# Attention with memory slots, a two-layer net and four experts: another layout for a softmax, and a new issue order

## The chip, the cores and the metric

The kernel runs on one core of a Trainium2 chip, as one launch. The metric is the device time of that launch in microseconds (us). The kernel before took 1147.62 us (median of 3 runs, 1147.52 to 1148.19). Five engines work side by side, each through its own queue strictly in order: TensorE (PE, with PEld for its weight loads), VectorE (DVE), ScalarE (ACT), GpSimd (POOL), and SyncE (SP), which here only issues DMAs. Results of PE land in PSUM; everything else lives in SBUF.

## The reference, cut to what matters

```python
# 4 batches x 8 heads, 576 tokens, head size 64, 32 memory slots
a = exp(phi - max over tokens); a /= sum over tokens + 1e-9      # first softmax, per head and slot
k_m, v_m = a^T k, a^T v                                          # 32 x 64 per head
scores = q k_m^T / 8;  attn = softmax over the 32 slots          # second softmax, per token
x = attn v_m                                                     # (2304 tokens, 512)
h = x @ w_in;  x = (max(h,0) + alpha*min(h,0)) @ w_out           # 512 -> 2048 -> 512 ("first layers")
p = domain_probs / sum
out = sum over 4 experts e of p[:, e] * (max(x @ w1[e], 0) @ w2[e])   # 512 -> 1024 -> 512
```

## The kernel before, in words

Precision first, since it sets how much PE has to do: most products are made of three passes in a fast fp32 type, with each operand split into a high part (a cast, on ACT) and a low part (the rest, `sub_to`, L140, on DVE or POOL). A product of two 128-wide blocks with 288 token columns is therefore three matmuls, and every operand has a "hi" and a "lo" that must exist before it.

The work falls into four stages.

- **Attention** (L160 to L321), per batch b and half g of the heads (4 heads x 32 slots = 128 partitions). `att_max`, `att_exp`, `att_sum` are the first softmax over the tokens, with phi laid out slots by tokens. `att_nat` turns the exponentials into the tokens' layout (four PE transposes a half and two more for the last 64 tokens), `att_natc` copies them out of PSUM on ACT, `att_mem` makes k_m and v_m from them, `att_memc` scales them by 1/sum, `att_memt` and `att_memtc` transpose those, `att_score` gives the scores of 288 tokens, `att_evac` takes them into the tokens' layout. Class `Soft` (L267) is the second softmax: max, sub, exp, sum, mul, back, and a split.
- **First layers** (class `First`, L446): 128 steps (c, b, k, f): `up` (L463 or L466) makes 128 hidden units of 288 tokens, `relu` and `act` apply the slope, `fin` and `fin2` split, `down` (L497 or L500) adds them to four PSUM banks, `evac` adds the banks to y. w_in and w_out arrive as integers' halves and are put together by class `Decode`; v_m is folded into w_in (`fold`), so that attention's last product and w_in are one.
- **Experts, batches 0 and 1**, then **batches 2 and 3**: 8 groups g of 512 hidden units. `Up` makes the hidden block of a unit by seven block products in place of eight (p1 to p7, L700), with sums v1, v16, v167 and blocks c11 to c22 between; `gate` applies max and p; `hi` and `lo` split; `Down` or `Seven` (L791, L831) makes the output. Weight splits made in the first half (`w1_hi`, `w1_lo`, `w2_split`, `s_sum`, `s_part`) are stored to HBM and loaded in the second.

What sets the order: everything is issued by hand. `ORDER` (L29) is a list of task names; each is one function call, and an instruction stands on its engine's queue where its task stands in the list. After the list, `run_experts` (L898) issues the experts by a fixed rule: around each product of a unit it calls `extra(place)` for the weight work of that place. `ON_VECTOR` (L95) names the low parts, subtractions and decode steps that go to DVE; the others go to POOL. `warm` (L148) issues matmuls on the identity whose result nobody reads; there are 42 of them, in tasks w0 to w3, all before the first transposes. Buffers come from pools with fixed counts: six PSUM banks for attention, sums and y (`ps_a`), two for hidden blocks and outputs (`ps_h`), three for raw weights (`rawp`), so a load or a product also waits until its buffer's last reader is done.

Of the kernel before, what the change touches and what calls it, by code (L numbers as in the profile page):

```python
# [8 lines left out]
F32 = mybir.dt.float32  # L9
# [15 lines left out]
NG = E * F // 512  # L25
UNIT = 4 * S
# [3 lines left out]
ppr w3 w1 w2 p0 a00_max rin0 rin1 w0 a00_exp a00_sum a01_max pal kv0 in0_1 in0_0 in1_1 pgates a01_exp a01_sum in1_0  # L30
in1_2 in1_3 in1_4 a00_nat a00_natc in0_2 a01_nat a01_natc a01_nath a01_nathc a00_mem p1 a00_memc a10_max a01_mem
a00_memt a01_memc a01_memt a01_memtc q0 a01_sc0 a11_max a00_memtc a00_sc0 a11_exp a01_ev0 s010_max in0_3 in0_4 f000
s010_sub s010_exp q01 a00_sc1 a01_sc1 a00_ev0 s000_max s000_sub a11_sum rin2 in2_1 in2_0 in2_2 in2_3 a10_exp a11_nat
# [71 lines left out]
def memory_attention_experts(ctx: ExitStack, tc: tile.TileContext, phi, q, kv, w_in, w_out, w1, w2, alpha, dp, out):  # L105
# [63 lines left out]
    def load_q(b, hf=None):  # L169
        if not hf:  # L170
            q_t[b] = unit(f"q{b}")
# [1089 lines left out]
```

## Time and profile before

| | |
|---|---|
| median of 3 runs | 1147.62 us |
| the profiled execution: its own time | 1150.11 us |
| its span, first to last instruction | 1148.3 us |
| PE busy | 1128.2 us, 98% |
| DVE, POOL, ACT busy | 72%, 42%, 38% |
| mean granted TensorE clock | 0.991 of full |
| attention and first layers | to about 388 us |
| experts, batches 0 and 1; 2 and 3 | to about 797 us; to the end |

"Busy" for PE is a share of time in which some matmul was under way, not the share of its peak. Matmuls are pipelined, so 12 of them show 1.6 us while one alone shows 0.3. A better measure of lost time in a stretch is how many matmuls of the same shape it held.

### The profile page before, as it was taken

The page shows a single profiled execution, that of the slowest core. Times are in us where ns is not written, and L with a number is a line of the kernel's source. Part 1 is how long each engine was busy: PE and PEld are TensorE (multiplying, and loading weights), DVE is VectorE, ACT ScalarE, POOL GpSimd, SP SyncE. Part 2 cuts the span into 40 slices and gives each one's busy share as a digit, 9 for nine tenths or more (in the row PEclk, how much of TensorE's full clock was granted, in tenths as well). Part 3 has the DMA queues.
Part 4 walks back from the last instruction along what each step waited for, and adds up shares of the span by engine and source line. Part 5 has one row for each costly group of instructions (what it writes and reads, how often), then busy time and mean ns, then how long its engine had stood idle before and what let it go on. Part 6 is the DMA issues. An engine that isn't in the chain of part 4 may idle for free.

```text
span 1148.3 us, 21977 instructions
## 1 busy us (share of the span) xinstructions
PE 1128.2 (98%) x8708; PEld 1086.3 (95%) x8708; DVE 822.8 (72%) x1498; ACT 441.0 (38%) x914; POOL 485.7 (42%) x395
## 2 busy tenths in 40 slices
PE   8999999999999989999999999999999999999998
PEld 7578999999999889999999999999999999999998
DVE  5998878675676565775766757687577777777794
ACT  4667644443444344333333333333532222222220
POOL 3345444342244574564745547333323333333320
PEclk9999999999999989999999999999999999999999
DMA  9552222111021273663745637585464555556522
GB/s 379 196 239 61 68 80 75 38 38 37 2 85 54 76 268 149 240 236 112 285 154 224 231 140 271 204 292 190 155 184 151 182 173 178 166 167 185 166 66 73
DMA packets 64214, 180.02 MB, mean 157 GB/s; under 512 B 6640, under 2 KB 23024, under 8 KB 60400
## 3 DMA queue, kind: packets, MB, share of 16 engines
q1 hardware_dynamic: 64112, 178.63, 45.0%
q8 instruction: 68, 1.11, 0.4%
q14 instruction: 34, 0.28, 0.1%
HBM read 114.34 MB, written 64.26 MB: 156 GB/s over the span
## 4 chain that ended last, share of the span: by engine, by line
PE 86%; DVE 5%; issue 1%; POOL 1%; DMA 1%; ACT 1%; DVEq 0%; ACTq 0%; POOLq 0%
PE o L808 18%; PE y L500 16%; PE c L872 13%; PE uy L700 12%; PE h L466 8%; PE ux L700 8%; PE uw L700 8%; PE pw L425 1%; PE y L497 1%; DVE g L140 1%; DMA kv<-in_kv 1%; POOL w L140 0%; POOL g L140 0%; DVE h L778 0%; PE pm L228 0%
## 5 line engine op out<-in xcount | busy, mean ns | idle before, releaser
L808 PE MATMUL o<-g,w 128*128 128x288 f32 x1536 | 225.8, 296 | 0.6 <-DVE g L140 0.3
L808 PEld LDWEIGHTS o<-g,w 128*128 128x128 f32 x1536 | 211.7, 189 | 1.1 <-DVE g L140 0.6
L500 PE MATMUL y<-g,wout 128*128 128x288 f32 x1440 | 207.3, 297 | 2.2 <-DVE g L140 1.9
L500 PEld LDWEIGHTS y<-g,wout 128*128 128x128 f32 x1440 | 196.5, 189 | 9.4 <-DVE g L140 2.4
L700 PE MATMUL uy<-x,w 128*128 128x288 f32 x1152 | 186.4, 297 | 2.9 <-DVE v L734 2.9
L700 PEld LDWEIGHTS uy<-x,w 128*128 128x128 f32 x1152 | 164.1, 189 | 5.3 <-DVE v L734 5.3
L872 PE MATMUL c<-gc,w2c 128*128 128x288 f32 x1008 | 156.5, 295 | 0.5 <-ACT acc L885 0.5
L140 POOL TENSOR_TENSOR gc<-h,gc 128x576 fp32r<-128x576 f32 x56 | 82.9, 1488 | 143.6 <-ACT gc L859 98.6
L872 PEld LDWEIGHTS c<-gc,w2c 128*128 128x128 f32 x1008 | 141.2, 188 | 1.0 <-ACT acc L885 1.0
L700 PE MATMUL ux<-x,w 128*128 128x288 f32 x768 | 124.2, 298 | 2.8 <-ACT v L738 2.8
L700 PE MATMUL uw<-x,w 128*128 128x288 f32 x768 | 122.7, 295 | 0.0
L140 POOL TENSOR_TENSOR g<-act,g 128x288 fp32r<-128x288 f32 x67 | 57.6, 863 | 140.8 <-ACT g L485 117.4
L700 PEld LDWEIGHTS ux<-x,w 128*128 128x128 f32 x768 | 110.2, 190 | 3.3 <-ACT v L738 3.3
L466 PE MATMUL h<-a,wp 128*128 128x288 f32 x720 | 111.2, 297 | 0.0
L140 POOL TENSOR_TENSOR w<-raww,w 128x512 fp32r<-128x512 f32 (+1 forms) x48 | 76.7, 1613 | 76.8 <-ACT w L602 49.8
L700 PEld LDWEIGHTS uw<-x,w 128*128 128x128 f32 x768 | 109.0, 188 | 0.0
L466 PEld LDWEIGHTS h<-a,wp 128*128 128x128 f32 x720 | 99.9, 188 | 7.5 <-DVE act L481 2.8
L859 ACT CAST gc<-h 128x576 fp32r<-128x576 f32 x70 | 47.3, 676 | 151.8 <-DVE h L851 138.4
L825 DVE TENSOR_TENSOR acc<-o,acc 128x288 f32<-128x288 f32 x112 | 50.8, 454 | 69.1 <-PE o L808 69.1
L481 DVE SCALAR_TENSOR_TENSOR act<-neg,bet,h 128x288 f32<-128x288 f32 x120 | 59.9, 510 | 52.3 <-ACT neg L472 45.3
L734 DVE TENSOR_TENSOR v<-uy,v 128x288 f32<-128x288 f32 x128 | 58.2, 454 | 53.2 <-PE uy L700 53.1
L472 ACT ACTIVATE neg<-h 128x288 f32<-128x288 f32 x128 | 52.1, 412 | 94.0 <-PE h L466 90.1
(164 smaller groups left out, 1611.4 us busy)
## 6 DMA issues: line engine op xcount, KB each, us to landing
kw<-w SPq DMA_DIRECT2D x16, 1792.0 KB, 6.7
raww<-in_w SPq DMA_DIRECT2D x32, 512.0 KB, 4.2
w<-kw SPq DMA_DIRECT2D x32, 512.0 KB, 4.8
kS<-S SPq DMA_DIRECT2D x56, 256.0 KB, 4.4
w2c<-kS SPq DMA_DIRECT2D x28, 512.0 KB, 3.6
kw<-w SPq DMA_DIRECT2D x25, 512.0 KB, 2.6
w<-kw SPq DMA_DIRECT2D x48, 256.0 KB, 4.0
kv<-in_kv SPq DMA_DIRECT2D x8, 1152.0 KB, 8.2
```

The source lines that it names most:

```text
L140: eng.tensor_tensor(out=out, in0=in0, in1=in1.bitcast(F32), op=ALU.subtract)
L425: mm(pw_t[b, c, u, n0][32 * t:32 * t + 32, 0:n1 - n0], vt_t[b, u][r, 32 * t:32 * t + 32], win_t[c][r, t, n0:n1], start=True, stop=True,)
L466: mm(p, wp_t[b, c, g][:, x, fs], a_t[b][:, y, g, o:o + HB], start=(n == 0), stop=(n == 5))
L472: nc.scalar.activation(out=self.neg, in_=self.p, func=AF.Relu, scale=-1.0)
L481: nc.vector.scalar_tensor_tensor(out=self.g, in0=self.neg, scalar=bet[:, ft:ft + 1], in1=self.p, op0=ALU.mult, op1=ALU.add)
L500: mm(First.acc[d], w[:, x, d * 128:(d + 1) * 128], self.gt[:, y, 0:HB], start=(self.start and n == 0), stop=(self.stop and n == 2))
L700: mm(p, w[:, x, a, k], operand(self.b, i)[:, y, k], start=(start and n == 0), stop=(n == 5), skip_group_check=not start)
L734: nc.vector.tensor_tensor(out=out, in0=x, in1=y, op=ALU.add)
L808: mm(self.p, w[:, x, i, d % 2 * 128:(d % 2 + 1) * 128], g, start=(m == 0), stop=(m == 11), skip_group_check=len(hps) == 1)
L825: nc.vector.tensor_tensor(out=a, in0=self.p, in1=a, op=ALU.add)
L859: nc.scalar.copy(out=t[:, 0], in_=self.raw[q])
L872: mm(self.p, w[:, x, i, m * 128:(m + 1) * 128], self.g_t[q][:, y, i], start=(k == 0), stop=(k == 5))
```

## The change

Three things, and an order that is new almost everywhere before the experts' second group and near the end.

1. For batches 2 and 3 (`b >= TURNED`), phi is loaded twice: in the slots' layout as before (into the other half of the buffer) and in the tokens' layout (`load_nat`, a host-side rearrangement of the same numbers). The column of negated maxima is turned into a row by one PE transpose a half (`att_row`), DVE adds it to the tokens' layout (`att_less`, one operand in PSUM), and ACT takes the exponential there (`att_nat`). The ten transposes a batch and their copies go. `att_exp` stays, for the sum.
2. For batches 1 to 3 the scores of both halves g are one task (`att_scores`); instructions are the same.
3. `run_experts` becomes `plan_experts`, which lists the same calls as named tasks, cut finer (`w1_lo` in two, a store apart from its split). `ORDER` now reaches into that list: the first expert units of groups 0 and 1 and the last ones of groups 5 to 7 are written out in `ORDER`; what stands between them keeps the old rule's order. `ON_VECTOR` is drawn anew. `bet`'s slope correction is a task of its own (`slopes`), and the combination of the seven products may run on POOL.

Warm-up matmuls are 72 in place of 42, in 24 tasks of three. By kind, the built program has on PE 20 transposes of exponentials fewer (40 to 20), 4 of maxima more, and 30 warm-ups more. DVE loses 29 instructions (1500 to 1471), POOL gains 37 (400 to 437), ACT 2, SP two DMAs (phi's second layout, 576 KB each). Of what goes from DVE to POOL, most is four `sub` and four `mul` of 128 x 576 and one of each of 128 x 288 in the second softmax, and five w_in products (with five more ACT conversions).

The diff, cut to its core (the two tables are shown by two lines each):

```diff
@@ ORDER, ON_VECTOR
-ppr w3 w1 w2 p0 a00_max rin0 rin1 w0 a00_exp a00_sum a01_max pal kv0 in0_1 in0_0 in1_1 pgates a01_exp a01_sum in1_0
+w1 w3 w0 w5 w18 p0 a01_max a00_max w8 w20 a01_exp a01_sum w17 a00_exp rin2 w14 w12 ppr in2_0 in2_1 w11 a00_sum rin0
...
+x1h5 e123 sp2 h126 h127 to x1l5 x1l6 p1_000 v1_000 wh01 l127 wl010 d124 d125 vh011 v16_000 x1h2 x1h4 l126 wl011 x1l2
@@ loads
     def load_phi(b):
-        pe_t[b] = unit(f"pe{b}")
-        nc.sync.dma_start(out=pe_t[b][:, 0:S2], in_=phi[b])
+        if b not in pe_t:
+            pe_t[b] = unit(f"pe{b}")
+        o = 0 if b < TURNED else S2
+        nc.sync.dma_start(out=pe_t[b][:, o:o + S2], in_=phi[b][:, S2:])
+
+    def load_nat(b):
+        if b not in pe_t:
+            pe_t[b] = unit(f"pe{b}")
+        nc.sync.dma_start(out=pe_t[b][:, 0:S2], in_=phi[b][:, 0:S2])
@@ first softmax (att_nat, att_natc of before are now att_turn, att_turnc, for b < 2)
+    def att_row(b, g):
+        p = pn_t[b, g] = bank(f"pn{b}{g}")
+        nc.tensor.transpose(p[:, 0:128], stats[b, g][1].to_broadcast([128, 128]), ident)
+
+    def att_less(b, g):
+        pe, p = pe_t[b], pn_t[b, g]
+        x = pe[:, g * 512:(g + 1) * 512].rearrange("p (c m) -> p c m", c=4)
+        nc.vector.tensor_tensor(out=x, in0=x, in1=p[:, 0:128].rearrange("p (c m) -> p c m", c=1).to_broadcast([128, 4, 128]), op=ALU.add)
+        r = slice(64 * g, 64 * g + 64)
+        nc.vector.tensor_tensor(out=pe[r, 1024:1152], in0=pe[r, 1024:1152], in1=p[r, 0:128], op=ALU.add)
+
+    def att_nat(b, g):
+        x = pe_t[b][:, g * 512:(g + 1) * 512]
+        nc.scalar.activation(out=x, in_=x, func=AF.Exp, scale=1.0)
...
+    def att_scores(b, hf):
+        for g in range(2):
+            att_score(b, g, hf)
@@ experts
-    def w1_lo(g, hp):
-        for (w, src), eng in zip(w1_parts(g, hp), (nc.gpsimd, nc.vector)):
-            sub_to(eng, w[:, 1], src, w[:, 0])
-        raw_t.pop(("w1", 2 * g + hp))
...
+    def w1_lo(g, hp, i):
+        w, src = w1_parts(g, hp)[i]
+        sub_to(engine(f"wl{g}{hp}{i}"), w[:, 1], src, w[:, 0])
...
-    def run_experts():
+    def plan_experts():
+
+        plan = []
+
+        def do(name, fn, *args):
+            plan.append((name, fn, args))
...
-    for i, n in enumerate((11, 12, 6, 13)):
-        task(f"w{i}", warm, n)
+    for i in range(24):
+        task(f"w{i}", warm, 3)
...
+    plan = plan_experts()
+    for name, fn, args in plan:
+        task(name, fn, *args)
...
         for name in ORDER.split():
             run(name)
-        run_experts()
+        for name, fn, args in plan:
+            if name in tasks:
+                run(name)
```

Three places of the new order, since the tables tell a reader little. **SP at the very start** (pe0 is phi of batch 0, rawin and rawout are chunks of w_in and w_out, kv00 and kv01 keys and values of batch 0). Before:

```order
L1123 DMA pr_104<-in_dp 128x72
L162 DMA pe0_150<-in_phi 128x1152
L335 DMA rawin0_155<-in_w_in 128x1024
L335 DMA rawin1_157<-in_w_in 128x1024
L1123 DMA bet_103<-in_alpha 128x16
L167 DMA kv00_178<-in_kv 128x2304
L167 DMA kv01_179<-in_kv 128x2304
L162 DMA pe1_246<-in_phi 128x1152
L173 DMA q0_286<-in_q 128x1152 x2
L335 DMA rawin2_340<-in_w_in 128x1024
L167 DMA kv10_380<-in_kv 128x2304
L167 DMA kv11_381<-in_kv 128x2304
```
Now:

```order
L331 DMA pe0_135<-in_phi 128x1152
L532 DMA rawin2_159<-in_w_in 128x1024
L1410 DMA pr_104<-in_dp 128x72
L532 DMA rawin0_180<-in_w_in 128x1024
L532 DMA rawin1_199<-in_w_in 128x1024
L1410 DMA bet_103<-in_alpha 128x16
L341 DMA kv00_253<-in_kv 128x2304
L341 DMA kv01_254<-in_kv 128x2304
L331 DMA pe1_280<-in_phi 128x1152
L347 DMA q0_322<-in_q 128x1152
L532 DMA rawin3_348<-in_w_in 128x1024
L347 DMA q0_322<-in_q 128x1152
```
A third w_in chunk stands ahead of the keys and values, and further on batch 1's keys and values now follow five loads that came after them before (a fourth w_in chunk, two of w_out's and both layouts of batch 2's phi: three of 512 KB and two of 576 KB).

**DVE where the first layers end** (act3313, g3313 are the last step's hidden block and its low part, y33100 to y33103 its sums; w101 is the second half of the first w1 block; v16000 and v167000 sums of the first expert unit). Before:

```order
L481 SCALAR_TENSOR_TENSOR act3313_4928<-neg3313_4894,bet_103,h3313_4880 128x288
L140 TENSOR_TENSOR w101_4986<-s01_4318,w101_4986 128x1024
L140 TENSOR_TENSOR g3313_4954<-act3313_4928,g3313_4954 128x288
L511 TENSOR_TENSOR y3_1782<-y33100_4912,y3_1782 128x288
L511 TENSOR_TENSOR y3_1782<-y33101_4913,y3_1782 128x288
L511 TENSOR_TENSOR y3_1782<-y33102_4914,y3_1782 128x288
L511 TENSOR_TENSOR y3_1782<-y33103_4915,y3_1782 128x288
L734 TENSOR_TENSOR v16000_5036<-uy000_5027,v1000_5034 128x288
L734 TENSOR_TENSOR v167000_5059<-uy000_5027,v1000_5034 128x288
L734 TENSOR_TENSOR h000_5051<-uw000_5038,v167000_5059 128x288
```
Now:

```order
L669 SCALAR_TENSOR_TENSOR act3313_4926<-neg3313_4923,bet_103,h3313_4909 128x288
L699 TENSOR_TENSOR y3_1815<-y33000_4847,y3_1815 128x288
L699 TENSOR_TENSOR y3_1815<-y33001_4848,y3_1815 128x288
L699 TENSOR_TENSOR y3_1815<-y33002_4849,y3_1815 128x288
L699 TENSOR_TENSOR y3_1815<-y33003_4850,y3_1815 128x288
L307 TENSOR_TENSOR x16_4900<-y1_1227,x16_4900 128x576
L307 TENSOR_TENSOR g3313_4960<-act3313_4926,g3313_4960 128x288
L307 TENSOR_TENSOR w101_5003<-raww11_3950,w101_5003 128x768
L921 TENSOR_TENSOR v16000_5038<-uy000_4828,v1000_5001 128x288
L307 TENSOR_TENSOR w101_5003<-s01_4368,w101_5003 128x1024
L699 TENSOR_TENSOR y3_1815<-y33100_5008,y3_1815 128x288
L699 TENSOR_TENSOR y3_1815<-y33101_5009,y3_1815 128x288
```
The low part of w101 stood ahead of the low part g3313 that the last `down` needs; now it stands behind it, cut in two, with the first expert sum between.

**ACT in the first expert units** (v1000, v1001, v1010 copy a first product out of PSUM, h000, h001 a block, g000, g001 are the high parts, w2000 to w2011 high parts of w2, S100 and S200 high parts of w2's sums). Before:

```order
L738 COPY v1000_5034<-ux000_5020 128x288
L753 COPY h000_5051<-ux000_5020 128x288
L784 CAST g000_5077<-h000_5051 128x576
L738 COPY v1001_5094<-ux001_5062 128x288
L784 CAST g000_5077<-h000_5051 128x576
L753 COPY h001_5114<-ux001_5062 128x288
L406 CAST w2000_5116<-raww20_4526 128x512
L406 CAST w2010_5121<-raww21_5017 128x512
L653 CAST S100_5137<-S10_5126 128x512
L653 CAST S200_5154<-S20_5141 128x512
L738 COPY v1010_5186<-ux010_5172 128x288
L784 CAST g001_5188<-h001_5114 128x576 x2
```
Now:

```order
L758 CAST x14_5041<-xt1_4710 128x576
L861 CAST w2000_5074<-raww20_5070 128x512
L861 CAST w2001_5076<-raww20_5070 128x512
L861 CAST w2010_5078<-raww21_4772 128x512
L758 CAST x14_5041<-y1_1227 128x576
L944 COPY h000_5101<-ux000_4994 128x288
L925 COPY v1001_5153<-ux001_5124 128x288
L834 CAST S100_5169<-S10_5072 128x512
L944 COPY h001_5199<-ux001_5124 128x288
L925 COPY v1010_5221<-ux010_5138 128x288
L976 CAST g000_5234<-h000_5101 128x576
L976 CAST g001_5236<-h001_5199 128x576
```
The copy v1010 stood behind two parts of w2's sums; now one part stands ahead of it, and the high parts of w2 stand ahead of h000 and v1001.

## Rows read from the trace of the kernel before

**Rows 1.** The page, part 1: busy time, share, instructions.

```profile
PE 1128.2 (98%) x8708; PEld 1086.3 (95%) x8708; DVE 822.8 (72%) x1498; ACT 441.0 (38%) x914; POOL 485.7 (42%) x395
```

**Rows 2.** Stretches: length; PE, PEld, DVE, ACT, POOL busy; clock, DMA share, GB/s.

```profile
20.00:30.00 10.00, 7.68 (x118) 4.48 (x105) 9.36 (x27) 5.89 (x17) 3.83 (x5) 0.69 1.00 418
30.00:40.00 10.00, 8.66 (x73) 5.29 (x73) 8.34 (x20) 5.02 (x15) 2.86 (x4) 0.80 0.33 120
40.00:100.00 60.00, 58.23 (x506) 43.65 (x507) 56.63 (x107) 40.22 (x97) 26.00 (x23) 1.00 0.54 199
...
380.00:420.00 40.00, 33.76 (x216) 32.52 (x215) 25.08 (x34) 14.62 (x29) 24.58 (x17) 0.87 0.54 200
450.00:470.00 20.00, 19.37 (x143) 18.83 (x142) 17.26 (x21) 8.52 (x17) 15.40 (x12) 1.00 0.86 322
510.00:740.00 230.00, 230.00 (x1730) 229.30 (x1729) 155.61 (x257) 76.27 (x133) 130.62 (x106) 1.00 0.54 203
1100.00:1120.00 20.00, 18.86 (x139) 18.18 (x138) 19.15 (x35) 4.43 (x9) 2.86 (x2) 1.00 0.06 20
```

**Rows 3.** Waits of PE, 376 to 412 us: waiter, releaser, total, times, longest.

```profile
PE ux L700 <- ACT v L738: 2.8, 1, 2.8
PE y L500 <- DVE g L140: 1.9, 1, 1.9
PE uy L700 <- DVE v L734: 1.5, 2, 0.9
```

**Rows 4.** Timeline of DVE, 364 to 386 us: start, us, line, operation, count, idle.

```profile
369.67 0.46 DVE L140 TENSOR_TENSOR g<-act,g 128x288 fp32r<-128x288 f32 x1 [0.50 <-ACT g L485]
...
381.60 2.05 DVE L140 TENSOR_TENSOR w<-s,w 128x1024 fp32r<-128x1024 f32 x1 [2.24 <-ACT w L602]
383.57 1.65 DVE L140 TENSOR_TENSOR g<-act,g 128x288 fp32r<-128x288 f32 x1
```

**Rows 5.** Timeline of all engines, 400 to 409 us, same columns.

```profile
405.01 0.62 ACT L653 CAST S<-S 128x512 fp32r<-128x512 f32 x1 [0.72 <-POOL S L644]
...
405.54 0.39 ACT L738 COPY v<-ux 128x288 f32<-128x288 f32 x1
...
405.99 1.68 PE L700 MATMUL ux<-x,w 128*128 128x288 f32 x6 [2.84 <-ACT v L738]
```

**Rows 6.** Timeline of PE, 0 to 80 us, same columns.

```profile
1.36 12.22 PE L153 MATMUL warm<-ident 128*128 128x128 f32 x84 [1.36 <-POOL ident masks.py:199]
...
24.79 4.96 PE L228 MATMUL pm<-kv,pe 128*32 128x128 f32 x80 [0.19 <-ACT pe L203]
30.17 4.12 PE L463 MATMUL h<-pe,wp 128*128 128x288 f32 x8 [0.41 <-DVE pe L311]
...
44.62 2.10 PE L463 MATMUL h<-pe,wp 128*128 128x288 f32 x8
...
61.64 0.60 PE L199 MATMUL pn<-ident,pe 128*128 128x128 f32 x4
...
65.19 2.80 PE L228 MATMUL pm<-kv,pe 128*32 128x128 f32 x80
```

**Rows 7.** Groups by line and shape: busy us, mean ns, idle, releasers.

```profile
L140 DVE TENSOR_TENSOR wp<-pw,wp 128x512 fp32r<-128x512 f32 x30 | 20.1, 680 | 2.7 <-ACT wp L438 2.7
...
L378 DVE SCALAR_TENSOR_TENSOR sin<-rawin,sin 128x512 f32<-128x512 uint32 x11 | 8.5, 775 | 0.2
...
L376 POOL TENSOR_TENSOR sin<-rawin,sin 128x512 f32<-128x512 f32 x5 | 7.4, 1470 | 13.0 <-DVE sin L371 10.7 <-PE pc L260 2.3
...
L305 DVE TENSOR_TENSOR pe<-pe,rs 128x576 f32<-128x576 f32 x4 | 3.6, 910 | 0.1
...
L288 DVE TENSOR_TENSOR pe<-pe,mx 128x576 f32<-128x576 f32 x4 | 3.3, 821 | 0.1
...
L305 POOL TENSOR_TENSOR pe<-pe,rs 128x576 f32<-128x576 f32 x2 | 2.8, 1414 | 0.5 <-PE h L466 0.5
```

**Rows 8.** DMA issues by line: count, KB, median us to landing.

```profile
raww<-in_w SPq DMA_DIRECT2D x32, 512.0 KB, 4.2
```

More of the change, by code (lines that the diff above doesn't have):

```diff
@@ L25 @@
 NG = E * F // 512
+TURNED = 2
 UNIT = 4 * S
 ORDER = """
[L30 to L33 removed]
@@ L169, in load_q @@
     def load_q(b, hf=None):
-        if not hf:
+        if b not in q_t:
             q_t[b] = unit(f"q{b}")
@@ L321, in split2 @@
             sub_to(self.eng2, self.lo, self.at, self.hi)
-    raw_order = [(kind, i) for g in range(NG) for kind in ("w1", "w2") for i in (2 * g, 2 * g + 1)]
-    raw_t, n_raw = {}, [0]
+    raw_t = {}
     def load_one(kind, i):
@@ L655, in s_part, with s_keep @@
             sub_to(nc.vector, t, src[0], src[1])
-        nc.sync.dma_start(out=kept_t["w2", g, n][:, part], in_=t.bitcast(F32))
+    def s_keep(g, n, part):
+        if ("w2", g, n) not in kept_t:
+            kept_t["w2", g, n] = dram.tile([128, 2, 512], F32, name=f"k{n}{g}")
+        nc.sync.dma_start(out=kept_t["w2", g, n][:, part], in_=cs_t[g, n][1 + part].bitcast(F32))
     def c_load(g, q):
@@ L1000, in run_experts, with s_do, up @@
             ups = [Up(g, b, hp) for hp in range(2)]
+            c = None
+            if ups[0].seven:
+                c = Seven(g, b, n_seven, ups)
+                n_seven += 1
+            def s_do(x, *what):
+                for w in what:
+                    kind, q = w[0], int(w[1])
+                    name = f"{kind}{x.g}{x.b}_{q}"
+                    if kind == "S":
+                        do(name, x.sum, q)
+                    elif kind == "H":
+                        do(name, x.hi, q)
+                    else:
+                        lo(name, x.lo, q)
             for hp, u in enumerate(ups):
                 seven = u.seven
+                def up(*names):
+                    for n in names:
+                        do(f"{n}_{u.name}", getattr(u, n))
                 def extra(place):
@@ L1137, in memory_attention_experts @@
     task("pgates", gates)
-    for i in range(4):
-        task(f"rw{i}", load_raw)
-    task("wk", w1_keep, 0, 0)
+    task("pbet", slopes)
     for b in range(B):
         task(f"p{b}", load_phi, b)
+        if b >= TURNED:
+            task(f"pz{b}", load_nat, b)
         task(f"kv{b}", load_kv, b)
@@ L1149, in memory_attention_experts @@
             task(k + "sum", att_sum, b, g)
-            task(k + "nat", att_nat, b, g)
-            task(k + "natc", att_natc, b, g)
+            if b < TURNED:
+                task(k + "turn", att_turn, b, g)
+                task(k + "turnc", att_turnc, b, g)
+            else:
+                task(k + "row", att_row, b, g)
+                task(k + "less", att_less, b, g)
+                task(k + "nat", att_nat, b, g)
             task(k + "mem", att_mem, b, g)
@@ L1200, in memory_attention_experts @@
                 task(f"{kind}{i}_{x}", fn)
-    for hp in range(2):
-        task(f"ws0{hp}", w1_sums, 0, hp)
-        task(f"wh0{hp}", w1_hi, 0, hp)
-        task(f"wl0{hp}", w1_lo, 0, hp)
     task("pst", store_gates)
@@ L1207, in memory_attention_experts @@
     task("to", to_experts)
-    for b in range(2):
-        task(f"pg{b}", load_gates, 0, b)
+    plan = plan_experts()
+    for name, fn, args in plan:
+        task(name, fn, *args)
     with tc.manual_schedule():
```

685 lines of the change are left out of this document (453 added, 232 removed).

## The prediction

> **What bounds the kernel now.** The first thing to read is the line of busy shares: PE is busy for 1128.2 us, 98% of the span [rows 1]. A change can then gain only where PE is held up or slowed, and "busy" alone does not show that, so the second view is the table of stretches, where I count matmuls instead. From 510 to 740 us PE does 1730 matmuls in 230 us without a gap, 0.133 us each [rows 2]. By that pace 380 to 420 should hold 301 and holds 216: 85 x 0.133 = 11.3 us are lost. 450 to 470 holds 143 of 150 (1.0 us lost), 1100 to 1120 139 of 150 (1.5 us) [rows 2]. The start can't be counted so, since its matmuls have other shapes; there I read the granted clock, 0.69 from 20 to 30 and 0.80 from 30 to 40, and idle time, 2.3 and 1.3 us. From 40 to 100 PE is idle for 1.8 of 60 us while DVE is busy for 56.6 (94%) and POOL for 26.0 [rows 2]: there DVE feeds PE with hardly any slack.
>
> Third come the waits. From 376 to 412 PE waits 1.9 us for a low part g (L500), 2.8 for a copy v (L738), and twice, 1.5 together, for DVE's v (L734) [rows 3]; that is 6.2 of the 11.3, and the rest is the lower clock that goes with the holes (0.87 in this stretch [rows 2]). The timelines say why. DVE stands idle for 2.24 us for an ACT cast of w101, takes 2.05 us for its low part, and only then the low part that the last `down` needs [rows 4]. ACT casts a w2 sum that POOL had finished late, and behind it in the queue stands the 0.39 us copy v for which PE idles 2.84 us [rows 5].
>
> **The change part by part.** The sum is made against the profiled execution, 1150.11 us, which stands 2.5 us above the median of 1147.62; the same 2.5 come off at the end.
>
> *PE's own work.* 16 transposes net go. Four show 0.60 us as a group [rows 6], 0.15 each; lying among other matmuls rather 0.11 (0.44 between the start of the group at 61.64 and the next at 62.08): -1.8 us. Of 72 warm-ups 42 still stand before the first transposes. 84 records took 12.22 us for 42 warm-ups [rows 6], 0.29 each. Thirty more would be 8.7 us if all stood in PE's way; but nine stand ahead of the first `att_mem`, where PE waits for keys and values, and nearly all others between score and fold steps where PE waits for ACT and DVE (its idle 2.3 + 1.3 us of rows 2). I charge one microsecond, three or four of them. Term: -0.8, bounds -1.8 and +6.9 (-1.8 + 8.7).
>
> *The start, to 100 us.* A third w_in chunk now stands ahead of the first keys and values: 512 KB [rows 8] at the 418 GB/s of this stretch [rows 2] is 1.25 us, on the path, since k_m, the scores, the softmax and the first h follow from it. So the first h, at 30.17 [rows 6], comes at about 31.4. Batch 1's keys and values follow five more loads, 3 x 512 + 2 x 576 KB, 6.6 us at that rate. Their use was at 24.79 [rows 6]; now it stands behind the first h on PE, about 32, so most of the delay is covered; if the cover is gone, up to 5 us stay. Against that stand two gains. The first: h x8 took 4.12 us at the low clock and 2.10 later, pm x80 4.96 and 2.80 [rows 6]. That is 4.2 us of slow clock; warm-ups between the steps would keep PE at work where it idled before. I take about half, -2.2. The second: DVE loses four `sub` (0.82), four `mul` (0.91) and five w_in products (0.775) [rows 7], 10.8 us; it gains four `att_less`, at most 0.68 + 0.46 each by the low part out of PSUM [rows 7] and a 128 x 288 [rows 4], 4.6. So 6.2 us of 56.6 go and the 1.8 us of PE's idle time with them, less what POOL, slower for the same work (1414 against 910 ns, 1470 against 775 [rows 7]), hands over late: five products x 0.7 and eight softmax steps x 0.5 are 7.5 us longer latency, mostly for steps whose tokens are needed later. I take -1.5. Sum: +1.2 - 2.2 - 1.5 = -2.5. Bounds: -6.5 (4.2 and 1.8, plus 0.5 of idle, no delay) and +6 (the 1.25 and 5 of the loads, no gain).
>
> By the Trainium skill ("SBUF — State Buffer", section "🔬 SBUF: two separate sides") GpSimd and a VectorE operation that reads two SBUF operands exclude each other on a shared port, the loser blocked for its whole instruction. By that rule moving work to POOL takes back from DVE more than it relieves, and `att_less`, with one operand in PSUM, would be spared. Nothing in the sum rests on it; what the rows make of the same thing is the third rival below.
>
> *The transition, 380 to 420.* The low part g3313 now precedes w101's, so the 2.24 and 2.05 us ahead of it [rows 4] go and the last `down` waits only for ACT's cast: the hole of 1.9 closes. Ahead of the copy v1010 stands one sum's part in place of two, and POOL has made it earlier: of 2.8 perhaps 0.8 stays. What is late next: ACT now has w2's high parts ahead of h000 and v1001, and they need a raw w2 load that can start only after a spill and a buffer set free by DVE; 4.2 us to landing [rows 8] is what such a wait can cost, and I count 1.5. On DVE the sum v167000 stands behind a 2.05 us low part and four additions of 0.46 [rows 4]: a hole of about 1. These new holes are 0.8 + 1.5 + 1.0 = 3.3 us of the 11.3, so -8. Bounds: -11.3 (none is left) and -2 (only the 1.9 closes, the others take each other's place).
>
> *450 to 470 and the middle.* Group 2 on keeps its order: 0, with ±1 from the 1.0 us lost there.
>
> *The end.* From 1100 to 1120 DVE is busy for 19.15 of 20 us, POOL for 2.86, and PE loses 1.5 [rows 2]. Now some combinations and low parts go to POOL. I take most of it, -1.2; bounds -2.1 (0.6 more after 1130, an estimate at the same share) and +0.5 (a POOL step at 1.4 us for DVE's 0.9 [rows 7] is late by 0.5).
>
> *Sum:* -0.8 - 2.5 - 8 + 0 - 1.2 = -12.5; 1150.1 - 12.5 = 1137.6 as a profiled execution, 1135 as a median.
>
> **The rivals.**
>
> *The holes of the transition move, not close.* w2's high parts wait on ACT for the raw load, v1001 and h000 with them, and the clock stays low. For it: the load starts after `sp2`, and in before one such queue position cost 2.84 us [rows 5]. Against it: the waits named in rows 3 had their causes in positions that are changed. The transition then gives -3 in place of -8: 1140.
>
> *Every hole closes:* -11.3, start -6.5, end -2.1, transposes -1.8: -21.7, 1126. For it: PE has the next unit's products at hand. Against: three changes of order would all have to hit.
>
> *DVE and POOL shut each other out: slower.* In the trace a 128 x 288 low part takes 0.46 us on DVE alone and 1.65 in the stretch where POOL works beside it [rows 4]; so a collision costs 1.2 us. Fifteen instructions move to POOL at the start (eight of 128 x 576, two halves, five products). Each with one collision is 18 us on a DVE that has 56.6 - 6.2 = 50.4 of 60: 68.4, 8.4 us over. With the start at +8.4 in place of -2.5, the transition at its bound of -2 (its low parts lie beside POOL too) and the end at +0.5, the sum is -0.8 + 8.4 - 2 + 0.5 = +6: 1153.7. It makes the kernel slower from the point where start and transition together exceed about +4. Against it: the mean of DVE's `mul` is 910 and of its `sub` 821 ns [rows 7], with POOL busy for 43% of that stretch; if each collision cost 1.2 us, these means would lie nearer to 1.2 than to 0.8. So the average price is some tenth of a microsecond, and few instructions pay the whole. The Trainium skill's rule ("SBUF — State Buffer", cited above) is this rival in general; here single rows agree with it (1.65 us) and the means do not.
>
> *The change does not reach PE:* the loads' delay (+1.25 to +5) eats the transition's gain: 1147.
>
> **How the numbers follow.** Forecast 1135, 55%, with a range of its own of 1130 to 1140. Moved holes 1140, 21%. All close 1126, 11%. Lock 1153, 9%. No effect 4%. The range must leave out no more than 2 in 10: the low end 1126 takes half of the case in which all closes, the high end 1146 all of the moved holes; outside are about 6% below and 12% above. 0.2%, 2.3 us, is what can be told from no change: faster 55 + 21 + 11 less 1 for a tail of the moved holes, 0.86; same 0.05; slower 0.09.
>
> **What would show it right or wrong.** Right: 380 to 420 holds over 270 matmuls and its clock is above 0.95; the wait y <- g is gone; no pm or h group before 40 us takes twice its later time; DVE's share from 40 to 100 is under 90%; 1100 to 1120 holds 145 or more. Moved holes: PE waits there again, behind ACT's w2 casts or DVE's v167. Lock: DVE's 128 x 576 and 128 x 512 means go up past 1.1 us. Wrong altogether: the middle, 510 to 740, loses matmuls, or PE waits for pm's keys by more than 3 us.

## The result, and the profile after

The changed kernel takes 1129.09 us (median of 4 runs, 1128.83 to 1131.2), the kernel before beside it 1147.6: a ratio of 0.9842, 95% interval 0.9825 to 0.9859. That is 18.5 us less, where 12.6 were forecast; the time lies inside the range. The profiled execution took 1128.83 us with a span of 1126.7, so against the profiled execution of before the gain is 21.3 us by the execution's own time and 21.6 by the span; before's profile was 2.5 us above its median, so some of the gain in the tables below may be chance.

Where the time came from is read first from the stretches of the changed kernel (length, busy us and instructions of PE, PEld, DVE, ACT, POOL, granted clock, DMA share, GB/s), beside [rows 2]:

```profile
20.00:30.00 10.00, 8.59 (x105) 5.71 (x97) 9.11 (x25) 7.71 (x20) 5.85 (x8) 1.00 1.03 426
30.00:40.00 10.00, 9.62 (x141) 6.04 (x149) 9.40 (x26) 6.64 (x18) 6.72 (x8) 1.00 1.02 426
40.00:100.00 60.00, 59.86 (x563) 47.81 (x548) 49.01 (x104) 42.66 (x104) 37.02 (x33) 1.00 0.44 168
380.00:420.00 40.00, 40.00 (x301) 39.88 (x301) 28.41 (x42) 17.14 (x34) 27.21 (x20) 1.00 0.42 153
420.00:450.00 30.00, 28.40 (x215) 28.17 (x214) 18.98 (x27) 13.18 (x27) 21.50 (x16) 1.00 0.92 342
450.00:470.00 20.00, 20.00 (x152) 20.00 (x152) 13.30 (x23) 5.48 (x9) 8.82 (x8) 1.00 0.43 162
510.00:740.00 230.00, 229.78 (x1726) 228.89 (x1726) 160.30 (x261) 77.94 (x137) 125.87 (x99) 1.00 0.56 208
1100.00:1120.00 20.00, 20.00 (x153) 20.00 (x152) 14.86 (x29) 2.60 (x4) 0.00 (x0) 1.00 0.24 82
```

The clock is 1.00 from 20 to 40 us, where before it was 0.69 and 0.80. From 40 to 100 DVE is busy for 49.0 us in place of 56.6, POOL for 37.0 in place of 26.0. 380 to 420 is full (301 records of 301). 1100 to 1120 holds 153 in place of 139. The middle has not moved. Two stretches are worse. 420 to 450 holds 215, where a full one holds 226 and the one of before held 228. And 1060 to 1080 holds 146, where it held 153 before. This second one in the changed kernel:

```profile
1060.00:1080.00 20.00, 19.57 (x146) 19.27 (x145) 16.87 (x28) 5.19 (x10) 14.05 (x10) 1.00 0.54 183
```

and in the kernel before:

```profile
1060.00:1080.00 20.00, 20.00 (x153) 20.00 (x152) 14.94 (x31) 5.46 (x10) 7.45 (x5) 1.00 0.47 153
```

The waits of PE over the whole execution of the changed kernel (waiter, releaser, us in total, times, longest) say what the first of the two is:

```profile
PE o L1000 <- ACT acc L1015: 1.6, 1, 1.6
...
PE h L651 <- DVE pe L509: 1.1, 1, 1.1
PE pw L613 <- POOL win L587: 0.5, 1, 0.5
...
PE uy L887 <- DVE v L921: 0.4, 2, 0.2
```

The three waits of [rows 3] are gone or down to 0.4 us. A new one of 1.6 us stands at an `o` (a product of `Down`) that waits for ACT. The timeline of ACT and PE around it (start, us, engine, line, idle before and its end):

```profile
424.08 0.62 ACT L861 CAST w<-raww 128x512 fp32r<-128x512 f32 x1 [4.93 <-DMA raww<-in_w]
...
424.60 0.39 ACT L944 COPY h<-ux 128x288 f32<-128x288 f32 x1
424.89 0.40 ACT L1015 COPY acc<-o 128x288 f32<-128x288 f32 x1
...
425.35 1.86 PE L1000 MATMUL o<-g,w 128*128 128x288 f32 x12 [1.60 <-ACT acc L1015]
```

ACT sits for 4.93 us before a cast whose raw w2 load has not landed; behind it stand two copies out of PSUM that were ready, and PE needs the second one. The last `down`, in contrast, now runs straight into the experts' products, of which the first twelve records already stand ahead of it, at 359.59:

```profile
370.75 6.56 PE L688 MATMUL y<-g,wout 128*128 128x288 f32 x48
377.15 0.96 PE L887 MATMUL uy<-x,w 128*128 128x288 f32 x6
377.95 0.96 PE L887 MATMUL uw<-x,w 128*128 128x288 f32 x6
```

The same instants in both traces give the balance, in us of the two profiled executions (the start of the same record, counted within its kind from 0):

| instant | before | after | gained so far |
|---|---|---|---|
| first transpose | 13.42 | 12.63 | 0.8 |
| first h | 30.17 | 30.38 | -0.2 |
| 300th y record of the first layers | 133.74 | 125.75 | 8.0 |
| last record of the last `down` of the first layers | 387.53 | 377.02 | 10.5 |
| 168th record of the experts' `up` | 431.29 | 409.24 | 22.1 |
| 300th | 467.64 | 447.72 | 19.9 |
| 1344th (first of batches 2 and 3) | 768.39 | 748.42 | 20.0 |
| last matmul's end | 1145.11 | 1123.50 | 21.6 |

The first transposes are PE's first work behind the 42 warm-ups (84 records) that stand ahead in both kernels. The 0.8 gained up to there can't be told from chance: in nine executions of the changed kernel and of its variants with the same start these transposes begin anywhere from 12.5 to 13.5 us. Counted from them instead, the five executions whose programs are equal up to the last `down` (the changed kernel, e6, e8, e9 and e10) agree within 0.1 us: 364.3 to 364.4 us, where the kernel before took 374.1.

Most of the first gain arises between the first h and the 300th y. Of the 10.5 us at the last `down`, 3.0 are that `down` itself: before, its twelve records took 4.5 us from the first start to the last, now 1.5. The wait of 1.9 us and the lower clock behind it are gone. On the other side the twelve `up` records that now stand ahead of it are 1.6 us of work. So the start is worth 10.5 - 0.8 - 3.0 + 1.6 = 8.3 us. From the last `down` to the 300th `up` record 9.4 are gained, 1.6 of them by those twelve records, so the transition is worth 3.0 + 9.4 - 1.6 = 10.8. The 2.1 that seem to go back between the 168th and the 300th are mostly order: 276 records of PE lie between them now and 264 before, and twelve records are 1.6 us. Nothing moves in the middle, and 1.6 come at the end.

For the first 10.5 a second table adds up, by kind, the time from the start of each PE record to the start of the next, up to the last record of the first layers. A wait or a slow clock is then charged to the record that precedes it:

| kind | before: records, us | after: records, us | difference |
|---|---|---|---|
| warm-ups | 84, 12.1 | 144, 19.7 | +7.6 |
| transposes of exponentials and maxima | 40, 7.5 | 24, 3.1 | -4.4 |
| pm (k_m, v_m) | 320, 14.6 | 320, 10.9 | -3.6 |
| h of batch 0 | 32, 11.8 | 32, 8.5 | -3.3 |
| pc (scores) | 128, 8.1 | 128, 6.7 | -1.4 |
| h and y of the other batches, pt | 2176, 299.6 | 2176, 292.2 | -7.4 |
| y of batch 0, folds, time before the first record | 34.0 | 34.4 | +0.3 |
| `up` products issued early | 0 | 12, 1.6 | +1.6 |

Thirty more warm-ups are sixty records and take 8.4 us of PE; the 84 ahead of the first transposes took 0.8 less than before. What the sixty give back can't be told from this table, since the layout, the scores and DVE's relief lie in the same rows; e1 tells it.

The prediction's third rival, the lock between DVE and POOL, is read from the groups (mean ns behind the busy time) of the changed kernel:

```profile
L307 DVE TENSOR_TENSOR S<-S,S 128x512 fp32r<-128x512 f32 x28 | 29.6, 1055 | 1.3 <-ACT acc L1015 0.6 <-ACT S L834 0.2
...
L307 DVE TENSOR_TENSOR wp<-pw,wp 128x512 fp32r<-128x512 f32 x30 | 20.5, 682 | 5.5 <-ACT wp L626 5.5
...
L503 POOL TENSOR_TENSOR pe<-pe,rs 128x576 f32<-128x576 f32 x6 | 7.0, 1166 | 10.7 <-PE pw L613 5.6 <-DVE rs L497 2.9 <-ACT neg L660 1.1
...
L399 DVE TENSOR_TENSOR pe<-pe,pn 128x512 f32<-128x512 f32 x4 | 2.7, 680 | 0.3 <-PE pn L394 0.3
...
L401 DVE TENSOR_TENSOR pe<-pe,pn 64x128 f32<-64x128 f32 x4 | 1.1, 281 | 0.0
```

and of the kernel before:

```profile
L140 DVE TENSOR_TENSOR S<-S,S 128x512 fp32r<-128x512 f32 x28 | 31.1, 1111 | 3.6 <-ACT S L653 3.1
```

Two low parts of the same shape tell the collisions apart. That of wp reads one operand from PSUM, and that of a w2 sum, S, reads both from SBUF. In the changed kernel the 23 of 28 low parts of S that lie beside a POOL instruction take 1137 ns in the mean and the other five 678; for wp it is 681 beside POOL and 684 without. So DVE does pay for POOL where both its operands lie in SBUF, some 0.46 us a time here, and not where one lies in PSUM. But the price did not grow. POOL is busy for 44 us more than before (529.7 against 485.7), and the mean of S went from 1111 to 1055. An estimate from the same traces: what DVE's two-operand instructions take over the undisturbed time of their shape adds up to about 65 us before and 60 now, and in the first 100 us to 3.5 and 1.4. POOL's `mul`, at 1166 ns, is no slower than it was (1414 [rows 7]). The new `att_less`, with one operand in PSUM, takes 680 and 281 ns, 3.8 us in all for four.

### The profile page after: what moved, and what is told of

Same layout as the page of the kernel before. It is cut to its first block, busy times and chain, and to the rows that moved or that the text cites. A ratio compares the mean times of both kernels' runs of the same rounds, so it can differ in the third digit from the quotient of the medians.

```text
span 1126.7 us, 22094 instructions
## 1 busy us (share of the span) xinstructions
PE 1117.2 (99%) x8752; PEld 1082.7 (96%) x8752; DVE 797.8 (71%) x1469; ACT 440.8 (39%) x916; POOL 529.7 (47%) x432
## 4 chain that ended last, share of the span: by engine, by line
PE 95%; DVE 2%; POOL 1%; issue 1%; DMA 0%; ACT 0%; POOLq 0%; DVEq 0%; ACTq 0%
PE o L1000 19%; PE y L688 17%; PE c L1060 13%; PE uy L887 13%; PE h L654 9%; PE uw L887 8%; PE ux L887 8%; PE y L685 1%; PE pw L613 1%; PE warm L320 1%; PE pm L422 1%; PE h L651 1%; PE pc L454 0%; POOL w L307 0%; DMA raww<-in_w 0%
## 5 line engine op out<-in xcount | busy, mean ns | idle before, releaser
L1000 PE MATMUL o<-g,w 128*128 128x288 f32 x1536 | 223.3, 295 | 1.6 <-ACT acc L1015 1.6
L307 POOL TENSOR_TENSOR g<-act,g 128x288 fp32r<-128x288 f32 x78 | 67.6, 873 | 121.1 <-ACT g L673 86.3
L307 POOL TENSOR_TENSOR w<-raww,w 128x512 fp32r<-128x512 f32 (+1 forms) x45 | 69.1, 1551 | 62.4 <-ACT w L791 38.9
```

What stands on the lines that cost most here:

```text
L307: eng.tensor_tensor(out=out, in0=in0, in1=in1.bitcast(F32), op=ALU.subtract)
L1000: mm(p, w[:, x, i, d % 2 * 128:(d % 2 + 1) * 128], g, start=(m == 0), stop=(m == 11), skip_group_check=len(hps) == 1)
```

## The experiments

All run one core, each beside the kernel before on the same chip. Where an edit undoes a part of the change, its price is taken from the traces: the time from the first transposes to the last record of the last `down`, 364.4 us in the changed kernel.

**Fewer warm-ups (e1).**

```diff
 ORDER
-... w9 ... w13 ... w2 ... w7 ... w21 ... w19 ... w10 ... w15 ... w22 ... w23
```


> The changed kernel with 42 warm-ups in place of 72: the first 14 groups stay, the three groups between the first transposes and att_mem and the seven later ones are left out. Theory A (the warm-ups between the steps hold the clock): the granted clock from 20 to 40 us falls from 1.0 to 0.7 to 0.85, h and pm groups there take near twice as long again, and the time rises by 2 to 5 us, to 1131 to 1134. Theory B (they only fill idle time, the clock is held by the new order of the real work): the clock stays at 1.0 and the time moves by less than 1 us, perhaps down, since 30 x 0.25 us of PE work go.

1129.71 us, 0.9831 (0.9816 to 0.9846) of before; the span is 1.1 us over the changed kernel's. Stretches of this run:

```profile
10.00:20.00 10.00, 7.87 (x132) 5.86 (x131) 8.22 (x13) 5.68 (x17) 5.86 (x4) 1.00 1.01 417
20.00:30.00 10.00, 5.97 (x60) 3.67 (x61) 9.43 (x26) 5.97 (x15) 6.53 (x8) 0.75 1.02 425
30.00:40.00 10.00, 10.00 (x125) 6.19 (x128) 6.82 (x19) 4.74 (x14) 5.61 (x6) 0.74 1.02 427
```

The clock falls to 0.75 and 0.74 as theory A says, so the warm-ups do hold it; it is at 0.50, the lower of its two levels (1.2 and 2.4 GHz), from 22 to 24 and from 29 to 35 us. PE had stood idle for 1.9 us up to 21.3 and for 2.0 up to 29.6. The price is smaller than A's 2 to 5 us. Behind the first transposes 8.4 us of warm-ups are gone and 9.9 come back in slower h, pm, scores, folds and in waits, a price of 1.4. By the medians and the ratios this run is not told from the changed kernel, as theory B has it for the time. Two of the waits are for q:

```profile
PE pc L454 <- DMA q<-in_q: 2.6, 2, 1.9
```

The kernel before has no such wait. Its two loads of q had landed by 16.3 and 18.5 us; with a third w_in chunk ahead of both and a fourth ahead of the second they land at 18.6 and 21.2 here. In the changed kernel warm-ups stand in that time. The keys and values land 1.3 us later than before as well, but pm does not wait for them. Counted from the first transposes pm starts at 1.8 us here, 0.6 of it a wait for a copy by ACT, at 1.3 before and at 3.2 in the changed kernel: there it is nine warm-ups that hold it up.

**Scores of the two parities apart (e2).**

```diff
-a2_sc1 s100_back a20_ev1 d4 a21_ev1
+a20_sc1 s100_back a20_ev1 d4 a21_sc1 a21_ev1
...
-a31_memtc n12 a3_sc0 a30_ev0 ... a3_sc1 a31_ev1
+a31_memtc a30_sc0 u12 n12 a31_sc0 a30_ev0 ... a31_sc1 a31_ev1 u14 a30_sc1
```


> The changed kernel with the scores of batches 2 and 3 issued one parity at a time again, another product of PE between them; instructions are the same. Theory A (two parities behind each other overlap on PE, since they use different rows of it: eight records take 0.62 us alone, 32 take 1.44 together): eight score groups take 0.62 each again and the time rises by 1.5 to 2.5 us, to about 1131. Theory B (as the prediction had it, the joint task changes nothing): the sum of the score groups of batches 2 and 3 stays at 2.9 us and the time within 0.5 us of 1129.1.

1132.39 us, 0.9858 (0.9841 to 0.9874); the price is 3.4 us. 2.0 of it are the score records themselves, 0.6 a transpose that now waits for DVE behind one group, the rest slower steps further on. PE's timeline in this run, two of its score groups:

```profile
62.52 0.69 PE L454 MATMUL pc<-q,kt 64*32 64x288 f32 x8
...
77.78 1.17 PE L454 MATMUL pc<-q,kt 64*32 64x288 f32 x16
```

PE's timeline in the changed kernel, its score groups of batches 1 to 3:

```profile
37.08 1.60 PE L454 MATMUL pc<-q,kt 64*32 64x288 f32 x32
...
56.30 0.86 PE L454 MATMUL pc<-q,kt 64*32 64x288 f32 x16
...
61.28 0.72 PE L454 MATMUL pc<-q,kt 64*32 64x288 f32 x16
...
74.77 1.51 PE L454 MATMUL pc<-q,kt 64*32 64x288 f32 x32
```

A parity here is a half g of the heads. Eight records alone take 0.69 us. Sixteen of one parity (the group at 77.78) take 1.17; sixteen of both parities take 0.72 and 0.86. The two parities use different halves of PE's rows (L454 takes rows 0 to 63 or 64 to 127) and overlap. The kernel before issued eight groups of eight for these two batches, as this run does. Theory A holds, and beyond its range: "instructions are the same" did not mean that the time is the same. The Trainium skill ("TensorEngine Tiling (Array Packing)", section "Key Properties") says that different tiles can load weights and multiply in parallel; the trace agrees, with 0.72 us for sixteen records against 1.17.

**The old layout of the first softmax (e3).** Tasks keep their places but for the exponentials, which moved behind the scaling of the batch before, and the load of batch 3's phi, which took the place of its second layout's.

```diff
-TURNED = 2
+TURNED = 4
 ORDER, for b = 2 and 3
-a{b}0_row a{b}1_row a{b}0_less a{b}1_less pz{b} a{b}0_nat a{b}1_nat a{b}1_nath
+a{b}0_turn a{b}0_turnc a{b}1_turn a{b}1_turnc a{b}1_turnh a{b}1_turnhc
```


> The changed kernel with the old way for batches 2 and 3: exponentials in the slots' layout, ten transposes a batch and their copies on ACT, no second phi load, no att_less. Theory A (the prediction's: the layout gives 16 transposes net, 1.8 us of PE, and costs DVE 4.6 us that are covered): +1.5 to +3 us, 1130.5 to 1132. Theory B (the layout gives nothing that lasts, as DVE pays for att_less what PE saves): -1 to +1. Theory C (a good part of the whole gain is the layout): over +5.

1135.74 us, 0.9888 (0.9873 to 0.9904): 7.5 us by the span, over theory A and at C. It has two parts. The price up to the last `down` is 4.0 us: 1.4 in the transposes, the rest in waits and in the steps that follow. Another 3.1 arise in the hole at 424 us, which grows. The longest wait of PE in this run:

```profile
PE o L1000 <- ACT acc L1015: 3.2, 1, 3.2
```

and the timeline of ACT at that place:

```profile
429.94 0.62 ACT L861 CAST w<-raww 128x512 fp32r<-128x512 f32 x1 [6.58 <-DMA raww<-in_w]
```

The clock from 420 to 450 is 0.94 here and 1.00 in the changed kernel, so about half of the 3.1 is the longer wait and the rest goes with the clock. The same raw load took 5.8 us from issue to landing here and 4.1 in the changed kernel, where it was issued 4.2 us sooner. Why it was slower was not found, so 4.0 us is what I put down to the layout, and even that holds the changed place of the exponentials.

**Softmax steps back on DVE (e4).**

```diff
 ON_VECTOR
+s000_sub s100_sub s110_sub s200_sub s300_sub in3_3 in5_3
```


> The changed kernel with the sub and mul of the five moved softmax halves and two w_in products back on DVE (4 x 0.82 + 4 x 0.91 + 0.9 + 2 x 0.78 = 9.4 us). Theory A (the start is bound by DVE, so the relief is what fills PE from 40 to 100): DVE goes from 49.0 to over 55 of 60 us there and the time rises by 2 to 6 us. Theory B (the order did it, DVE has slack): under 1 us either way. Theory C (POOL and DVE exclude each other on a shared port and the move cost more than it gave): the time falls by 1 us or more.

1133.07 us, 0.9863 (0.9848 to 0.9877), 4.4 us by the span. The price is 3.7 us. The first transposes of this execution began at 13.54, 0.9 later than those of the changed kernel, and that is not in the 3.7. The stretch from 40 to 100 in this run:

```profile
40.00:100.00 60.00, 58.57 (x545) 45.28 (x534) 53.88 (x110) 40.94 (x100) 27.99 (x24) 1.00 0.43 160
```

and two waits of PE:

```profile
PE h L639 <- DVE pe L497: 2.0, 1, 2.0
...
PE pn L382 <- DVE nm L344: 1.0, 1, 1.0
```

DVE's busy time goes from 49.0 to 53.9 us, and the first h waits 2.0 us for DVE in place of 1.1. Counted from the first transposes, the first h comes 1.0 us later, the 300th y 3.7. Theory A, though DVE stayed just under the 55 us that I had named; against C, the move to POOL gives here and does not take.

**Before, with the last low part first (e5).**

```diff
-x1h1 ... h127 to wh01 wl01 l127 d127
+x1h1 ... h127 to wh01 l127 wl01 d127
```


> The kernel before with one pair of tasks exchanged: w101's low part is issued behind the last low part g3313 in place of ahead of it. Theory A (position on DVE's queue is what held up the last down): the wait y <- g of 1.9 us goes from 380 to 420, and the time falls by 1.5 to 4 us, more than the wait where the clock stays up; the waits ux <- v and uy <- v stay. Theory B (the w101 part is then late itself and the first expert products wait for it): 0 to +1 us, with a new wait on w.

1145.52 us, 0.9974 (0.9965 to 0.9983): 2.8 us less by the medians, 4.2 by the span. The transition in this run:

```profile
380.00:420.00 40.00, 35.81 (x244) 34.81 (x244) 24.77 (x34) 16.66 (x32) 28.58 (x20) 0.91 0.55 207
```

and the waits of PE that are left there, over the whole execution:

```profile
PE ux L700 <- ACT v L738: 2.8, 1, 2.8
PE uy L700 <- DVE v L734: 2.8, 6, 0.8
```

The wait y <- g is not in the list any more, and 380 to 420 holds 244 records in place of 216, while the two other waits stay. Theory A. 28 records are 3.7 us: twice the wait of 1.9, since the clock stays higher (0.91 against 0.87). The last `down` alone takes 1.5 us in place of 4.5 from its first start to its last.

**The second group's w2 casts later (e6), and two warm-up groups fewer (e7).**

```diff
-rw22 ss1S1 vh100 vl100 wl110 wk11 p4_100 c11_100 c21_100 vk100 p1_101 F01_2 D01_1
+rw22 wl110 wk11 p4_100 c11_100 c21_100 p1_101 F01_2 ss1S1 vh100 vl100 vk100 D01_1
 in e7 besides
-w7 w21
```


> The changed kernel with the casts of the second group's raw w2 (and the sum of them) moved behind the next copies out of PSUM. Theory A (the only hole left, 1.6 us at 424, is ACT waiting for that load while a finished copy stands behind it): PE's wait o <- acc goes, the time falls by 1.2 to 2.2 us, to about 1127.3. Theory B (the w2 parts are then late for the products that need them): 0 or slower, with a wait of o on w.

> As the kernel before it in this list, and without two of the 24 groups of warm-ups, the two that stand between batch 0's transposes and its scores. Theory A (the clock holds without them and the first h comes up to 0.8 us earlier): 0.3 to 1 us faster than with them. Theory B (the clock falls to the low level from 20 to 40 us as with all ten left out): 0.5 to 1.5 us slower than with them.

1128.49 us, 0.983 (0.9814 to 0.9846), and 1129.1 us, 0.9836 (0.9822 to 0.9851), beside 0.984 (0.9825 to 0.9854) for the changed kernel itself (next run). Waits of PE in e6:

```profile
PE ux L887 <- ACT v L925: 1.0, 1, 1.0
```

The wait o <- acc is gone and one of 1.0 us for a copy v has come in its place, since that copy stands behind the casts now. By the instants the stretch from the 168th to the 300th `up` record takes 37.9 us in place of 38.5. So A names the right cause, but the cast only moved its wait; the gain of 0.5 us is not told from no change. In e7 the first h comes at 30.04 against 30.38 and 31.26 (changed kernel, e6), a spread that arises ahead of the first transposes. Counted from these, e7's last `down` comes 0.2 us sooner than e6's (364.2 against 364.4), and its clock from 20 to 40 us is 1.00 in both stretches. So the clock holds without these two groups, and they are worth 0.2 us at most: neither theory's size.

**The changed kernel again (e8).**

> The changed kernel once more, beside the others of this call, so that differences of a few tenths of a per cent are taken on one chip: ratio to the kernel before 0.984, span 1126.7 us within 0.5.

1129.03 us, 0.984 (0.9825 to 0.9854), span 1126.9.

**A sum ahead of the copy again (e9).**

```diff
-p6_010 v1_010 ... ss0S2 sq0S20
+p6_010 ss0S2 sq0S20 v1_010
```


> The changed kernel with one more sum of w2 (S20, on POOL) and its cast on ACT issued ahead of the copy v1010, as in the kernel before. Theory A (that position is what cost the 2.84 us wait of before): PE waits 1 to 4 us for v near 395 to 402 and the time rises by 1 to 4 us, more than the wait if the clock falls. Theory B (in the new order POOL has the sum in time): under 0.5 us.

1128.76 us, 0.983 (0.9815 to 0.9845). Timeline of ACT in this run:

```profile
399.98 0.63 ACT L834 CAST S<-S 128x512 fp32r<-128x512 f32 x1
400.50 0.40 ACT L925 COPY v<-ux 128x288 f32<-128x288 f32 x1
```

The cast S runs without idle time and the copy follows it: POOL has the sum ready. Theory B. In the kernel before, ACT had stood idle for 0.72 us for that sum [rows 5], and for longer ahead of the sum in front of it:

```profile
403.67 0.62 ACT L653 CAST S<-S 128x512 fp32r<-128x512 f32 x1 [4.64 <-POOL S L644]
```

So what cost 2.84 us there was, by these rows, sums that POOL made too late, not the place of one 0.6 us cast. No run moves POOL's sums in the kernel before, so this is argued from the rows and not shown by an edit.

**Combinations on DVE (e10).**

```diff
 ON_VECTOR
+cb20 cb22 cb23 cb31 cb32
```


> The changed kernel with the five combinations of outputs that run on POOL put back on DVE (5 x 0.8 us or so). Theory A (the 1.5 us lost from 1100 to 1120 before came from DVE, and moving work off it gave the gain at the end): +0.7 to +2 us, with PE waiting for DVE at the end. Theory B (the order near the end gave it): under 0.5 us.

1130.41 us, 0.9844 (0.983 to 0.9859), 1.6 us by the span over e8. Two stretches near the end in this run:

```profile
1060.00:1080.00 20.00, 18.93 (x140) 18.40 (x139) 17.78 (x30) 5.05 (x9) 8.16 (x6) 1.00 0.54 185
...
1100.00:1120.00 20.00, 19.82 (x150) 19.59 (x149) 15.58 (x30) 2.60 (x4) 0.00 (x0) 1.00 0.24 81
```

and the wait of PE that is new:

```profile
PE uw L875 <- DVE h L909: 0.6, 1, 0.6
```

PE waits 0.6 us for DVE's h, at 1075.72, and 1060 to 1080 holds 6 records fewer than in the changed kernel; 1100 to 1120 loses 3. Theory A by the size, which is that of the 1.6 us found at the end. But the holes are not those of before: there PE waited for DVE from 1103 to 1113 us and at 1134, and 1060 to 1080 was full. So it is shown that these five steps on DVE cost 1.6 us in the new order, and not that they alone are the gain over the kernel before.

**All four parts of the start undone (e11).**

```diff
 the edits of e1, e2, e3 and e4 together
```


> The changed kernel with all four parts of the start undone at once: 42 warm-ups, scores of batches 2 and 3 apart, the old layout, softmax steps and two w_in products on DVE; the new order of tasks stays. One by one their end of the first layers came later by 1.1, 3.4, 4.3 and 4.6 us, 13.4 in sum, while the whole change took 10.5 from there, 1.9 of it the wait of the last down. Theory A (they are separate costs on PE and add up; the new order by itself loses some 4 us at the start): +12 to +15 us at the end of the first layers. Theory B (they share one slack, DVE and the chains behind it, so that undoing one uncovers what another hid): +7 to +10. Theory C (the order is tuned to them and stalls without them): over +16.

1138.83 us, 0.9926 (0.9901 to 0.9951). The price is 10.8 us. Two stretches of this run:

```profile
20.00:30.00 10.00, 5.34 (x58) 3.06 (x58) 9.30 (x26) 5.47 (x15) 2.85 (x4) 0.76 1.03 426
40.00:100.00 60.00, 57.36 (x527) 41.30 (x528) 47.44 (x93) 37.42 (x95) 26.30 (x23) 1.00 0.38 140
```

and its longest waits of PE:

```profile
PE h L639 <- DVE pe L497: 3.5, 1, 3.5
PE pc L442 <- DMA q<-in_q: 3.0, 2, 1.9
```

One by one the parts cost 1.4 + 3.4 + 4.0 + 3.7 = 12.5 us, together 10.8. That falls between A and B: they share a little, the rest adds up. Without the four, the way from the first transposes to the last `down` is 375.2 us, 1.6 of them the twelve `up` records; the kernel before takes 374.1, 3.0 of them the hole in its last `down`. So the new order of the start loses some 2.5 us by itself. Part of this shows as the 3.0 us in which PE waits for q, as in e1. It is not a wait for the keys and values: pm starts at 14.27 here.

## Why the prediction was right, and which terms were off

- **PE's own work and the start** (-0.8 and -2.5, together -3.3; measured -8.3). The direction of each piece that had one was right and the size was not. This is the term that was mis-sized. *Scores:* costed at nothing, because the instructions are the same; worth 3.4 (e2). That step failed. *DVE's relief:* 1.5 forecast, 3.7 measured (e4). I had let it pay only for the 1.8 us in which PE is shown idle from 40 to 100; e4 shows that it pays 1.0 before the first h already, and the rest in waits spread over the steps after it. *The layout:* 1.8 us of transposes less what DVE pays; 4.0 measured with the reservations above (e3), since the copies on ACT and the chain behind them go too. *Clock:* 2.2 us back for 1.0 of warm-ups; measured 9.9 for 8.4 (e1). That the difference of 1.4 is near the 1.2 forecast is luck, with both sides far larger. The nine warm-ups ahead of `att_mem` were taken to stand where PE waits for keys and values; without them pm starts 1.4 us sooner behind the first transposes. *The w_in chunk:* forecast at +1.25 through keys and values. They do land that much later (the second at 14.70, before at 13.45), but PE does not wait for them; it waits for q (2.6 us in e1, 3.0 in e11). The new order as a whole loses some 2.5 (e11). Batch 1's keys did not hold up PE.
- **The transition** (-8; measured -10.8: 3.0 in the last `down`, 7.8 behind it). All of the wait named in [rows 4] went, and e5 shows that this exchange alone was worth 3 to 4 us with the clock that goes with it. The holes that I left, 0.8 for the sum and 1.0 for v167000, did not appear (e9: POOL has the sum). The third, ACT before a w2 load, did, one group later: 4.93 us on ACT and 1.6 on PE, with the clock at 1.00 from 420 to 450. That is the first rival's mechanism at a fraction of its price.
- **The middle** (0): from the 300th to the 1344th record of `up` 300.75 us before and 300.70 now. Right.
- **The end** (-1.2; measured -1.6). Right in size. That work off DVE is what gives it fits e10, which costs as much; but e10's holes lie elsewhere, and the changed kernel has a new one of 0.6 us at 1065.
- **The lock** (the slower rival, 9%): it did not make the kernel slower, but it is there on average, and the prediction's reading that the means do not agree with it was wrong. The row to take is one with both operands in SBUF: S, at 1111 ns before and 1055 now, against 680 and 682 for wp. The Trainium skill's rule on the shared port ("SBUF — State Buffer", section "🔬 SBUF: two separate sides") names just these, a VectorE operation with two SBUF inputs against a GpSimd one that reads SBUF; the trace agrees, with 1137 ns beside POOL and 678 without. What the rule does not give is the step to "takes back from DVE more than it relieves": e4 would then have been faster, and it was 3.7 us slower.
- Of the signs that the text asked for, those on 380 to 420, on y <- g, on h and pm before 40 us, on DVE's share (82%) and on 1100 to 1120 came as written.

The sum, -12.5, was too small because the two largest terms were both too careful. Between the profiled executions the gain is 21.6, by the medians 18.5; the first is the -21.7 of the case in which every hole closes. That is partly luck: 0.8 of the 21.6 is chance ahead of the first transposes, and that case gave the start its 8.3 us (6.5 and 1.8) through the clock, DVE's idle time and the transposes, with nothing for the scores.

## What to carry to other kernels

Measure a stage by instants that both traces share, not by busy shares: PE was idle for 1.8 us from 40 to 100, and 8.2 were gained between the first h and the 300th y. Start counting behind the part that chance moves: here the first transposes. Products that use different halves of PE's rows cost little behind one another (0.72 to 0.86 us for two groups of eight) and full price when something stands between (0.69 each), so the order of equal instructions has a price of its own. When a hole at a stage's border closes, look at the load that the next group's cast waits for: a cast on an in-order queue passes its wait to every copy behind it. And to see whether POOL slows DVE, compare rows of one shape with both operands in SBUF and with one in PSUM; a mean over the wrong rows shows nothing.

## What the runs showed of the hardware

- Sixteen score records of 64 x 32 tiles take 0.72 or 0.86 us when they use both row halves, 1.17 when they use one; eight alone take 0.69 (e2).
- A low part of 128 x 512 on DVE with both operands in SBUF takes 678 ns, and 1137 in the mean beside a POOL instruction; with one operand in PSUM it takes 684 and 681.
- The clock from 20 to 40 us was 1.00 with warm-ups between the steps, also with two groups fewer (e7), and 0.73 to 0.76 without ten of the groups (e1, e11); PE had idled 2.1 and 4.0 us of the 10 to 20 and 20 to 30 stretches in e1. That cost 9.9 us in slower steps and waits together, not the 4.2 that I had read from two groups.
- The 42 warm-ups ahead of the first transposes gave way to these anywhere from 12.5 to 13.5 us in nine executions with the same start.
- The same 512 KB load took 4.1 us in one program and 5.8 in another at the same place in the order; the cause stays open.
